# Token-major query features and a deferred layer-norm scale in a four-layer linear-attention and GLU kernel

## The chip, the cores and the metric

The kernel runs on one core of a Trainium2 chip. The metric is the device time in microseconds of that core; the median of several executions is quoted. The engines are called PE (TensorE matmul), PEld (its weight load), DVE (VectorE), ACT (ScalarE), POOL (GpSimd) and SP (SyncE, which here does nothing but issue DMAs). The granted clock is the share of PE's full clock that the profile shows as passed by the throttle. The record marks an execution as slow when it is over 1.5% above the fastest of the same kernel.

## The reference, cut to what matters

2048 tokens (16 tiles of 128), width 512, 32 heads of 16, GLU width 1376, bf16. Layers 1 and 3 are attention, 2 and 4 are GLUs; every layer reads a layer norm of x and adds to x.

```python
phi_q = concat([softmax(pq), softmax(-pq)], -1)     # pq = q @ w_phi per head, 16 -> 32 features
phi_k = concat([softmax(pk), softmax(-pk)], -1)
kv  = einsum("bhsf,bhsd->bhfd", phi_k, v);  z = einsum("bhsf->bhf", phi_k)
num = einsum("bhqf,bhfd->bhqd", phi_q, kv)
den = einsum("bhqf,bhf->bhq", phi_q, z)[..., None] + 1e-6
o   = (num / den) @ wo
...                                                  # GLU: (relu(x @ Wg) * (x @ Wu)) @ Wd
x = x + A(ln(x)); x = x + B(ln(x)); x = x + A(ln(x)); x = x + B(ln(x))
```

`kv` sums over all tokens. So each attention layer has a barrier: nothing of `num` can start before the last tile's k features have been accumulated. The stretch from that last accumulation to the first GLU matmul is called the boundary here; there are two, near 54 to 72 us and near 239 to 257 us.

## The kernel before

The program records every operation with its reads and writes in a list. A list scheduler then orders each engine's instructions by a model of their durations; a priority grows with the place in the emission, so what is emitted earlier tends to run earlier. Twenty stored steps of a random search improve that order. The program hands each engine, and the SP queue of DMA issues, its instructions in that order.

```python
# before: q is projected feature-major (features on partitions, tokens along the free dimension),
# so exp(q) can be the weights of num at once. A softmax sum over features is then a sum over
# partitions, which num computes itself: 144 columns = 128 of kv, 8 of den, 8 of the softmax sums.
op("pe", matmul(pb[bank][:, j*GW:(j+1)*GW], expq[:, st, c, s, tt*128:(tt+1)*128], kvbd[:, g0+j, :]))  # GW = 144
...                       # 3 evictions per tile, then zm, zd, zr, ab, tsc, o on POOL and DVE
self.dma_tr(dma_start_transpose(oT[:, ob, :, :], osb[:, b, :]), ...)    # o of one tile, on the SP queue
for c in range(NC):
    op("pe", matmul(pb[bank][:], oT[:, ob, c, :], wo_p[:, c, :]), ...)
op("dve", tensor_tensor(x_sb[:, t, :], x_sb[:, t, :], pb[bank][:], ALU.add), ...)
...
def ln(t): stats, aggregate, rstd = (var + eps)^-0.5, y = (x - mean) * rstd, then dma_tr(yT <- y)
...
# order of emission in each attention layer
N([0, 1, 2, 3])                                       # num .. wo and layer norm of tiles 0 to 3
for st in range(1, NSLAB):
    self.q_proj(st, qring, A, ...)                    # q projection and exp of tiles 4 to 15
mix(steps_B([0, 1], HA), steps_N([4, 5]))             # GLU of tiles 0, 1 between N of 4, 5
...
```

All transposes in DMA (`dma_tr`) go through the one SP queue: 60 of y (the normalised x), 32 of o and 11 others, besides most of the loads and stores.

The softmax here doesn't subtract the row's maximum and nothing guards it: scores larger than these inputs give would overflow.

## Time and profile before

| | before |
|---|---|
| time, median | 394.94 us (393.89 to 395.74) |
| span of the profiled execution | 391.6 us, granted clock 0.999 |
| PE, DVE, ACT, POOL busy | 94%, 68%, 51%, 43% |

The page of the profile: busy time by engine; then PE's busy tenths and the granted clock in 40 equal slices; then the DMA queue of SP; then the engines' shares of the chain that ended last.

```profile
PE 369.0 (94%) x2336; PEld 201.8 (52%) x2379; DVE 268.1 (68%) x551; ACT 201.5 (51%) x381; POOL 170.2 (43%) x287
...
PE   5898988999999999999999997979999999999996
...
PEclk9999999999999999999999999999999999999999
...
q1 hardware_dynamic: 65328, 23.07, 26.3%
...
PE 84%; DMA 5%; DVE 4%; ACT 3%; issue 2%; POOL 1%; SPq 0%; POOLq 0%; DVEq 0%
```

PE is the bound: it works 94% of the span at full clock and makes up 84% of the chain. The two groups of the page that the change touches most (busy us, mean ns of one; then the idle time before them and its releaser):

```profile
L774 PE MATMUL ps<-wo_p,oT 128*128 128x512 bf16 x117 | 35.3, 379 | 3.9 <-DMA oT<-osb 3.5
...
L743 PE MATMUL ps<-kvbd,expq 128*128 128x144 bf16 x256 | 33.6, 226 | 2.4 <-DVE kvbd L716 2.1
```

A matmul's 226 ns isn't the spacing, since the next one starts before it ends. The timeline shows three num matmuls in a row in 0.35 us, so the spacing is (0.35 - 0.226) / 2 = 62 ns.

The table of stretches (us from start to end; busy us of PE, PEld, DVE, ACT, POOL; granted clock; DMA share; GB/s) at the two boundaries:

```profile
60.00:70.00 10.00, 8.82 (x57) 4.40 (x56) 8.60 (x22) 8.64 (x13) 3.97 (x10) 1.00 0.20 42
70.00:80.00 10.00, 9.04 (x78) 6.41 (x78) 8.42 (x22) 7.67 (x16) 7.98 (x18) 1.00 0.36 70
80.00:90.00 10.00, 9.57 (x68) 6.48 (x69) 8.05 (x20) 3.38 (x10) 5.17 (x10) 1.00 0.34 69
...
250.00:260.00 10.00, 6.89 (x48) 3.78 (x47) 7.85 (x17) 7.87 (x12) 7.01 (x14) 1.00 0.32 57
260.00:270.00 10.00, 9.95 (x89) 7.83 (x90) 7.85 (x22) 5.94 (x17) 6.46 (x14) 1.00 0.29 59
```

PE loses at most about three microseconds in a stretch of ten, and the clock stays at 1.00.

### The profile page before, as it was taken

Reading aid. Unit: us, or ns where it says so; the run is one execution under the profiler, and the core shown is the slowest. Engines: PE = TensorE matmul, PEld = TensorE weight load, DVE = VectorE, ACT = ScalarE, POOL = GpSimd, SP = SyncE. Lnnn points to the kernel's source line nnn. Section 1 sums busy time; section 2 is a strip of 40 time slices with the busy share of each in tenths; the row PEclk is TensorE's granted clock in tenths of the full one; section 3 lists DMA queues with packets and bytes.
Section 4 is the critical chain, followed back from the end, with each engine's and each line's share of the span. In section 5 each row is a group of like instructions: output and inputs, shape, how many; then the busy total and the mean of one; then the engine's idle time right before and its main releaser. Section 6 shows DMA issues by size and latency. Waiting matters only on the chain.

```text
span 391.6 us, 6419 instructions
## 1 busy us (share of the span) xinstructions
PE 369.0 (94%) x2336; PEld 201.8 (52%) x2379; DVE 268.1 (68%) x551; ACT 201.5 (51%) x381; POOL 170.2 (43%) x287
## 2 busy tenths in 40 slices
PE   5898988999999999999999997979999999999996
PEld 4444444576744554454444464456774445454443
DVE  5989878887766889766675776978875676322222
ACT  5787869742643413534354475965652561443340
POOL 7597952771543383533433652466544252000000
PEclk9999999999999999999999999999999999999999
DMA  6752492332221225301110120233233123100001
GB/s 195 195 80 57 114 364 53 70 65 47 54 51 29 41 54 83 68 2 27 27 15 0 27 28 2 41 62 68 62 69 79 27 43 83 41 13 15 27 28 55
DMA packets 66080, 24.08 MB, mean 61 GB/s; under 512 B 57888, under 2 KB 65024, under 8 KB 66048
## 3 DMA queue, kind: packets, MB, share of 16 engines
q1 hardware_dynamic: 65328, 23.07, 26.3%
q10 hardware_dynamic: 720, 0.59, 0.5%
q8 instruction: 19, 0.31, 0.4%
q14 instruction: 13, 0.11, 0.1%
HBM read 7.91 MB, written 2.10 MB: 26 GB/s over the span
## 4 chain that ended last, share of the span: by engine, by line
PE 84%; DMA 5%; DVE 4%; ACT 3%; issue 2%; POOL 1%; SPq 0%; POOLq 0%; DVEq 0%
PE ps L795 34%; PE ps L844 19%; PE ps L654 9%; PE ps L774 6%; PE ps L727 5%; PE ps L685 3%; PE ps L743 3%; PE ps L821 2%; DMA oT<-osb 2%; PE ps L699 2%; DMA yT<-ytile 1%; ACT expq L730 1%; DMA x_sb<-in_A_x_dram 1%; DVE tsc L763 1%; ACT expk L688 0%
## 5 line engine op out<-in xcount | busy, mean ns | idle before, releaser
L795 PE MATMUL ps<-yT,Wgu 128*128 128x512 bf16 (+1 forms) x789 | 173.8, 336 | 0.5
L795 PEld LDWEIGHTS ps<-yT,Wgu 128*128 128x128 bf16 x800 | 75.7, 98 | 62.0 <-ACT expk L803 1.4
L844 PE MATMUL ps<-Wd,hT 128*128 128x512 bf16 (+2 forms) x356 | 103.5, 373 | 0.4
L797 ACT ACTIVATE gate_sb<-ps 128x512 bf16<-128x512 f32 (+1 forms) x100 | 50.4, 513 | 82.7 <-PE ps L795 71.8
L673 POOL TENSOR_TENSOR expk<-expk,rZk 128x1024 bf16<-128x1024 bf16 (+1 forms) x32 | 59.6, 1876 | 33.1 <-DVE rZk L668 27.6
L844 PEld LDWEIGHTS ps<-Wd,hT 128*128 128x128 bf16 (+1 forms) x363 | 35.2, 98 | 35.8
L805 DVE TENSOR_TENSOR hT<-gate_sb,expk 128x512 bf16<-128x512 bf16 (+1 forms) x65 | 26.8, 422 | 29.4 <-ACT expk L803 23.4
L588 DVE BATCH_NORM_STATS2 stats<-x_sb 128x6 f32<-128x512 bf16 x64 | 42.6, 680 | 4.8 <-DMA x_sb<-in_A_x_dram 4.2
L401 ACT ACTIVATE numbf<-ps 128x432 bf16<-128x432 f32 x64 | 33.0, 539 | 20.1 <-PE ps L743 19.5
L666 DVE TENSOR_REDUCE Zk<-expk 128x64 f32<-128x1024 bf16 x32 | 38.1, 1205 | 4.5 <-ACT expk L688 2.6
L846 DVE TENSOR_TENSOR x_sb<-x_sb,ps 128x512 bf16<-128x512 bf16 (+1 forms) x33 | 22.0, 670 | 26.8 <-PE ps L844 26.6
L768 POOL TENSOR_TENSOR osb<-tsc 128x512 bf16<-128x512 bf16 x28 | 32.3, 1155 | 17.6 <-DVE tsc L763 17.6
L774 PE MATMUL ps<-wo_p,oT 128*128 128x512 bf16 x117 | 35.3, 379 | 3.9 <-DMA oT<-osb 3.5
L727 PE MATMUL ps<-yT,Wqp 128*128 128x512 bf16 x123 | 34.6, 379 | 2.3 <-ACT expq L730 2.1
L730 ACT ACTIVATE expq<-ps 128x1024 bf16<-128x1024 f32 (+1 forms) x40 | 32.2, 861 | 7.2 <-PE ps L727 5.9
L743 PE MATMUL ps<-kvbd,expq 128*128 128x144 bf16 x256 | 33.6, 226 | 2.4 <-DVE kvbd L716 2.1
L595 POOL TENSOR_SCALAR rv<-mv 128x1 f32<-128x1 f32 (+1 forms) x53 | 12.6, 240 | 53.6 <-DVE mv L590 53.1
L803 ACT ACTIVATE expk<-ps 128x512 bf16<-128x512 f32 (+1 forms) x65 | 32.2, 501 | 6.3 <-PE ps L795 6.2
L596 POOL TENSOR_TENSOR rstd<-rv,mhalf 128x1 f32<-128x1 f32 (+1 forms) x53 | 31.5, 597 | 3.0
L631 DVE TENSOR_SCALAR ytile<-x_sb,mv,rstd 128x512 bf16<-128x512 bf16 x52 | 22.1, 426 | 12.4 <-POOL rstd L596 11.7
L754 POOL TENSOR_TENSOR zm<-numbf 128x64 f32<-128x64 bf16 x28 | 10.5, 375 | 45.8 <-DVE numbf L401 33.0
L657 ACT ACTIVATE expk<-ps 128x512 bf16<-128x512 f32 x44 | 23.7, 603 | 12.5 <-PE ps L654 12.0
(78 smaller groups left out, 428.9 us busy)
## 6 DMA issues: line engine op xcount, KB each, us to landing
out_dram<-x_sb SPq DMA_DIRECT2D x15, 128.0 KB, 1.7
x_sb<-in_A_x_dram SPq DMA_DIRECT2D x3, 512.0 KB, 6.4
Wgu<-in_B_W_gate_dram SPq DMA_DIRECT2D x4, 344.0 KB, 4.0
Wgu<-in_B_W_up_dram SPq DMA_DIRECT2D x4, 344.0 KB, 5.9
Wd<-in_B_W_down_dram SPq DMA_DIRECT2D x5, 256.0 KB, 7.7
yT<-ytile SPq DMA_TRANSPOSE x60, 2.5
hT<-in_A_wqkv_dram ACTq DMA_DIRECT2D x4, 128.0 KB, 3.0
x_sb<-in_A_x_dram SPq DMA_DIRECT2D x4, 128.0 KB, 3.5
```

Of the source, the lines that this page charges most:

```text
L401: return e.activation(out, in_, ACT.Copy) if hasattr(e, "activation") else e.tensor_copy(out, in_)
L588: op("dve", (lambda t: lambda e: e.bn_stats(k.stats6[:, t, :], k.x_sb[:, t, :]))(t), [r("x", t)], [r("st", t)], 685, f"{tag} stats {t}")
L654: op("pe", (lambda ic, bank, W: lambda e: e.matmul(k.pb[bank][:], k.yT[:, ic, t * 128:(t + 1) * 128], W[:, ic, :], start=(ic == 0), stop=( ...
L666: op("dve", lambda e: e.tensor_reduce(k.Zk[:, zb, :], k.expk[:, t, :, :, :].rearrange("p g s (h f) -> p (g s h) f", f=16), AX.X, ALU.add), ...
L673: op(eng, (lambda kv, u0, n: lambda e: e.tensor_tensor(kv, kv, k.rZk[:, rb, u0 * 32:u0 * 32 + n].unsqueeze(2).to_broadcast([P, n, 16]), AL ...
L727: op("pe", (lambda c, ic, bank: lambda e: e.matmul(k.pb[bank][:], k.Wqp[:, ic, c * 128:(c + 1) * 128], k.yT[:, ic, st * 512:(st + 1) * 512 ...
L730: op("act", (lambda c0, s, b0: lambda e: e.activation(k.expq[:, st, c0:c0 + w, s, :], k.ps[:, b0:b0 + w, :], ACT.Exp, scale=(1.0 - 2.0 * s ...
L743: op("pe", (lambda s, c, j, g0, bank: lambda e: e.matmul(k.pb[bank][:, j * GW:(j + 1) * GW], k.expq[:, st, c, s, tt * 128:(tt + 1) * 128], ...
L774: op("pe", (lambda c, bank: lambda e: e.matmul(k.pb[bank][:], k.oT[:, ob, c, :], k.wo_p[:, c, :], start=(c == 0), stop=(c == NC - 1)))(c, ...
L795: op("pe", (lambda bank, W, ic, fc, Mf: lambda e: e.matmul(k.pb[bank][0:Mf, 0:n], W[:, ic, fc * 128:fc * 128 + Mf], k.yT[:, ic, c0:c0 + n] ...
L797: op("act", (lambda Mf, gb, gs: lambda e: e.activation(k.gate_sb[0:Mf, gs, 0:n], k.pb[gb][0:Mf, 0:n], ACT.Relu))(Mf, gb, gs), [self.RP[gb] ...
L844: op("pe", (lambda fc, Kf, u, c0, bank, m0, m1: lambda e: e.matmul(k.pb[bank][:, m0:m1], k.hT[0:Kf, u, c0:c0 + 128], k.Wd[0:Kf, fc, m0:m1] ...
```

## The change

Two things are changed. First, q is projected token-major. The softmax sums are then ordinary sums along the free dimension, and num shrinks from 144 to 68 columns (4 heads of 16 and their den). But num contracts over features, so the features must be transposed back: two DMA transposes of 128x512 per tile and layer, 64 in all. Second, the layer norms before layers 2 to 4 are deferred: `512 x - sum(x)` is transposed at once, while the scale is computed beside it and enters later, at the exp, at the copy of v, or at the GLU's residual (relu(s g) * (s u) = s^2 relu(g) u). The stored search steps, which belonged to the old program, are gone. Smaller things come with it: the ring of oT has 3 buffers instead of 4, and num keeps one pair of PSUM banks for every tile.

```diff
-    STEPS = (540311766, 892937877, ... 18 more ...)
+    STEPS = ()
-GW = 144
+HW = 17
+GW = 4 * HW
...
-    def q_proj(self, st, ring, tag, after=(), w=1):      # out = Wqp^T @ yT : feature-major
+    def q_proj(self, ts, ring, tag, scaled=False):       # out = yT^T @ Wqp : token-major
...
+        for tt in ts:
+            self.qnorm(tt, tag)
+    def qnorm(self, t, tag):
+        op("dve", tensor_reduce(Zq[:, b, :], expq[:, t, ...], AX.X, ALU.add), ...)
+        op("dve", reciprocal(rZq, Zq of exp(q)), ...)
+        op("pool", tensor_tensor(rho, rZq, Zq of exp(-q), ALU.mult), ...)
+        for u in range(2):
+            op("pool", tensor_tensor(exp(q) half u, same, rho, ALU.mult), ...)
+            self.dma_tr(dma_start_transpose(qT[:, tb, u*4:u*4+4, :], expq[:, t, u*4:u*4+4, :, :]), ...)
...                                                        # num: 8 matmuls of 68 columns from qT
-        # three evictions, zm, zd, zr, ab, tsc, o
+        op("dve", reciprocal(rden, den in PSUM), ...)
+        op("dve", tensor_tensor(osb, num in PSUM, rden, ALU.mult), ...)
...
+    def center(self, t, tag, power):
+        op("dve", tensor_scalar(ytile, x, 512., sx, op0=ALU.mult, op1=ALU.subtract), ...)
+        self.dma_tr(dma_start_transpose(yT[...], ytile), ...)
+        op("act", activation(sq, x, ACT.Square, scale=-512., bias=sx, accum_out=vx), ...)
+        ...                                                # rx = (vx/512 + eps*512^2)^power on POOL
...
             N([0, 1, 2, 3])
-            for st in range(1, NSLAB):
-                self.q_proj(st, qring, A, ..., w=2)
+            for t in range(4, NT, 2):
+                self.q_proj([t, t + 1], qring, A, last)    # with qnorm and both transposes of t, t+1
             mix(steps_B([0, 1], HA), steps_N([4, 5]))
```

## The prediction

> **What bounds the kernel now.** TensorE. The page gives PE 369.0 us of a 391.6 us span (94%) at granted clock 0.999, and the chain that ended last is 84% PE. From 90 to 220 us and from 260 to 380 us the table of stretches shows PE busy 9.9 of every 10 us. PE idles at the start, at the first attention-to-GLU boundary (50-90 us: 4.2 us), at the second (220-260 us: 5.5 us) and in the tail. DVE, ACT and POOL have slack on average, but in 36-54 us POOL is busy 16.2 and DVE 15.4 of 18 us.
>
> **Removed from PE.** The 256 "num" matmuls shrink from 144 to 68 columns. In the timeline six in a row take 0.54 us, the first 0.226, so 63 ns apiece; 27 k-v accumulations of 65 columns with their own 128-column weights take 0.86 us, 32 ns apiece. So 256 x 31 ns = 8 us less. Given back: four eps matmuls (0.5 us), and 68 instead of 65 columns (0.3 us). Net about 7 us, nearly all on the chain.
>
> **Moved on the other engines (estimates from the group means).**
> - ACT loses 64 num evictions (33 us), gains 48 Square passes of about 0.9 us and slower one-tile exps with a per-row scale: +20 us, mostly where it has room.
> - DVE loses num casts 14, tsc 22, zr 11, and stats and aggregation for 48 tiles (41); gains Zq 39, rZq 11, rden 13, o from PSUM 22, row sums 4: about even.
> - POOL: slightly less.
> - SP gains 64 transposes at 1.19 us of issue each (+76 us on 121), 2.4 us to land.
>
> **The chains at the boundaries.** From the last k-v accumulation to the GLU: eight mask operations (2.4 us) become two, the seven steps from num to o become two (rden 0.42, o 0.7), and stats, aggregate, rv and rstd (1.7 us) leave: 3 to 5 us shorter per boundary. That isn't all gained, since q projections fill PE meanwhile.
>
> Second boundary: gain 2 to 3 us. First: about nothing, perhaps a loss, because the q normalisation of the first tiles (1.55 us DVE, 1.5 us POOL each) enters a stretch where both are full, and its transposes share the SP queue with 6 MB of late weights issued at 41-54 us (DMA share 0.98 in 50-60 us). The Trainium skill, "DMA: Bandwidth & Descriptors", section on queues, rings and completion order says descriptors on one engine's ring are consumed in order; a transpose behind the weights would land only at about 60 us.
>
> **Against it.** The twenty schedule-search steps, tuned for the old program, are gone: my guess is a loss of 1 to 4 us (no number in the trace sizes it).
>
> **Sum.** 395 - 7 (num) - 2.5 (second boundary) + 0.5 (first) + 2.5 (lost search) - 1.5 (shorter waits elsewhere) = about 387 us. 80% range 380.5 to 393.5. Chances: faster by over 2% 0.5, within 2% 0.46, slower by over 2% 0.04: the middle lies right on the border.
>
> **What would show it.** Num matmuls near 32 ns apiece; PE busy sum down by 7 to 15 us; PE still 9.9 of 10 in the GLU stretches; PE idle at the second boundary below 4 us; first num at 58-61 us instead of 56.8, waiting on a q transpose.
>
> **What would make it wrong.** A table load for each Square (1.28 us each); transposes queueing on SP so that num or wo waits for DMA in the GLU stretches; num's two banks, now held per tile until DVE has read them, stalling PE; a much worse order without the search; or, the other way, boundaries closing wholly (380 us).

## More of the kernel before

The SP queue at the first boundary, from the timeline (start us, time on the queue, line, what is issued, how many):

```profile
53.91 0.50 SPq L579 DMA_DIRECT2D Wd<-in_B_W_down_dram  x1
61.31 7.79 SPq L771 DMA_TRANSPOSE oT<-osb  x3
69.69 2.50 SPq L634 DMA_TRANSPOSE yT<-ytile  x2
72.58 4.36 SPq L771 DMA_TRANSPOSE oT<-osb  x2
```

Only seven transposes are issued from 54 to 76.9 us, and the queue rests in between.

## The result, and the profile after

The kernel after took 423.79 us (median of 4, 422.6 to 424.91) against 395.26 us for the kernel before in the same rounds. The ratio is 1.0727, 95% interval 1.0687 to 1.0768: slower. A ratio here is the mean time of one kernel's fast runs over that of the other's of the same rounds, so it is not quite the ratio of the medians quoted. The prediction of 387.0 us (380.5 to 393.5) was wrong in size and in direction.

The page after, the same lines:

```profile
PE 374.1 (89%) x2343; PEld 195.1 (46%) x2383; DVE 255.2 (60%) x507; ACT 215.0 (51%) x421; POOL 158.9 (38%) x288
...
PE   5898976399799999999999999739998999999996
...
PEclk9999999689899999999999999957999999999999
...
q1 hardware_dynamic: 100080, 31.47, 37.6%
...
PE 62%; DVE 15%; DMA 10%; SPq 5%; issue 3%; ACT 3%; POOL 2%; DVEq 0%; ACTq 0%
```

No engine is busier as a share of the span. What changed is that PE has two holes, in slices 7 and 8 and in slices 26 and 27, and that the granted clock falls with or just after them (slices 8 and 9, and 27 and 28; a third, smaller dip is in slice 11). SP's own queue, 0% of the chain before, is 5% of it, and DMA has doubled.

The groups: num costs 18.0 us of busy time instead of 33.6 (eight in a row take 0.41 us, so the spacing is (0.41 - 0.194) / 7 = 31 ns, as predicted). The new idle time stands before wo and before the GLU's first block, and both wait for a DMA transpose:

```profile
L804 PE MATMUL ps<-wo_p,oT 128*128 128x512 bf16 x125 | 39.5, 406 | 12.3 <-DMA oT<-osb 11.7
...
L850 PE MATMUL ps<-Wgu,yT 128*128 128x192 bf16 x128 | 17.4, 260 | 11.6 <-DMA yT<-ytile 11.6
```

PE's waits (what waited, for what: us in all, times, the longest) say how long each lasts:

```profile
PE ps L804 <- DMA oT<-osb: 11.7, 7, 5.3
PE ps L850 <- DMA yT<-ytile: 11.6, 6, 3.1
```

The stretches at the two boundaries:

```profile
60.00:70.00 10.00, 6.21 (x59) 3.20 (x60) 6.54 (x12) 4.57 (x5) 5.60 (x11) 1.00 1.00 207
70.00:80.00 10.00, 5.16 (x26) 1.62 (x24) 8.12 (x20) 5.01 (x9) 6.23 (x15) 0.88 0.47 93
80.00:90.00 10.00, 5.68 (x34) 3.95 (x35) 6.00 (x12) 2.30 (x7) 2.29 (x6) 0.61 0.65 105
...
270.00:280.00 10.00, 3.29 (x17) 1.08 (x16) 8.27 (x18) 4.43 (x10) 5.14 (x12) 0.78 0.50 95
280.00:290.00 10.00, 6.80 (x33) 4.53 (x35) 3.35 (x9) 2.88 (x9) 1.49 (x4) 0.54 0.60 91
```

And SP's queue at the first boundary:

```profile
66.80 1.27 SPq L801 DMA_TRANSPOSE oT<-osb  x1
68.17 2.51 SPq L783 DMA_TRANSPOSE qT<-expq  x2
70.74 1.26 SPq L801 DMA_TRANSPOSE oT<-osb  x1
72.17 2.50 SPq L783 DMA_TRANSPOSE qT<-expq  x2
74.72 1.27 SPq L801 DMA_TRANSPOSE oT<-osb  x1
76.09 2.52 SPq L783 DMA_TRANSPOSE qT<-expq  x2
78.66 1.26 SPq L668 DMA_TRANSPOSE yT<-ytile  x1
80.01 2.53 SPq L783 DMA_TRANSPOSE qT<-expq  x2
82.60 1.26 SPq L668 DMA_TRANSPOSE yT<-ytile  x1
```

Between two o transposes, and again between two y transposes, stand two q transposes for tiles that nobody needs yet, and the queue never rests: one start follows the other at 1.3 us. The o of a tile therefore comes every 3.9 us, and the GLU gets its first y at 81 us. The DMA engines themselves are half idle meanwhile (share 0.47 to 0.65). The queue that issues is full, and what lies behind it is not.

The holes then cost twice. The Trainium skill, "TensorE: Matmul & The Clock Gate", section "Part 1: The HAM clock gate", says that PE falls to half clock after an idle window of about 3.4 us and needs a busy one to come back. The trace agrees in kind, but not on the length. Stretches of one microsecond at the edges of the two large falls (the column before the last two is the clock):

```profile
77.00:78.00 1.00, 0.73 (x3) 0.36 (x4) 0.69 (x1) 0.42 (x2) 0.76 (x3) 0.81 0.63 130
78.00:79.00 1.00, 0.86 (x3) 0.00 (x0) 0.10 (x1) 0.00 (x0) 0.33 (x1) 0.50 0.40 81
...
87.00:88.00 1.00, 1.00 (x7) 0.56 (x5) 0.00 (x0) 0.50 (x2) 0.00 (x0) 0.57 0.30 62
...
275.00:276.00 1.00, 0.00 (x0) 0.00 (x0) 1.00 (x3) 0.00 (x0) 0.92 (x3) 0.80 0.31 61
...
289.00:290.00 1.00, 1.00 (x10) 0.84 (x9) 0.25 (x1) 1.00 (x4) 0.00 (x0) 0.88 0.67 130
```

At the first boundary the clock falls to 0.50 at 77.6 us, just after a wait of 2.5 us (it ended at 77.3), and is back at 87.9; the wait of 3.1 us, from 82.0 to 85.1, lies inside the fall and didn't start it. At the second it falls at 275.6 us, 3.7 us into the wait of 5.3 us, and is back at 289.2. A third fall, from 108.3 to 111.8 us, begins as a wait of 2.6 us ends. So waits shorter than the page's window were enough here. The slowest wo matmul takes 634 ns where the kernel before has at most 390. The half clock is most of why PE's busy time rose to 374.1 us although its work shrank: e18 below, with the same matmuls at full clock, has 366.4 us.

Where the span grew by 30.5 us, in milestones (start of each in the trace, us; the last two rows are explained below):

| | last k-v sum, layer 1 | first GLU matmul, layer 2 | last k-v sum, layer 3 | first GLU matmul, layer 4 | end |
|---|---|---|---|---|---|
| before | 54.1 | 72.2 | 238.8 | 256.6 | 391.6 |
| after | 62.8 | 81.2 | 260.8 | 281.2 | 422.1 |
| e7 | 59.3 | 76.5 | 242.3 | 254.8 | 386.9 |
| e18 | 59.5 | 74.0 | 243.6 | 256.6 | 388.8 |

From before to after: 8.7 us up to the first milestone, 0.3 to the second, 13.0 to the third, 2.5 to the fourth and 6.0 to the end. The loss isn't inside the boundary alone: while the backlog of q transposes lasts, the GLU that follows is starved too (PE busy 7.13 of 10 us at 100 to 110 us). A milestone isn't a fixed amount of PE's work, since the scheduler may move projections across it; the table says when, not why.

The 8.7 us before the first milestone are another loss than the queue at the boundary. From 33.5 to 54.4 us the chain of waits of the kernel after runs through DVE: the softmax sums of k, those of the first q tiles, and y. In the kernel before it is PE's own work for most of that time.

### The profile page after: what moved, and what is told of

It reads as the page before. It is cut to its first block, busy times and chain, and to the rows that moved or that the text cites. A ratio compares the mean times of both kernels' runs of the same rounds, so it can differ in the third digit from the quotient of the medians.

```text
span 422.1 us, 6512 instructions
## 1 busy us (share of the span) xinstructions
PE 374.1 (89%) x2343; PEld 195.1 (46%) x2383; DVE 255.2 (60%) x507; ACT 215.0 (51%) x421; POOL 158.9 (38%) x288
## 4 chain that ended last, share of the span: by engine, by line
PE 62%; DVE 15%; DMA 10%; SPq 5%; issue 3%; ACT 3%; POOL 2%; DVEq 0%; ACTq 0%
PE ps L824 27%; PE ps L873 16%; PE ps L804 6%; PE ps L683 6%; DVE Zq L772 4%; DMA yT<-ytile 4%; SPq L783 4%; DMA oT<-osb 4%; DVE Zk L696 2%; PE ps L850 2%; DVE stats L593 2%; PE ps L755 2%; PE ps L791 1%; PE ps L715 1%; POOL expk L703 1%
## 5 line engine op out<-in xcount | busy, mean ns | idle before, releaser
L826 ACT ACTIVATE gate_sb<-ps 128x512 bf16<-128x512 f32 (+1 forms) x100 | 50.4, 511 | 86.5 <-PE ps L824 78.7
L670 ACT ACTIVATE sq<-x_sb,sx 128x512 bf16<-128x512 bf16 x48 | 34.7, 724 | 47.1 <-DVE x_sb L657 42.6
L804 PE MATMUL ps<-wo_p,oT 128*128 128x512 bf16 x125 | 39.5, 406 | 12.3 <-DMA oT<-osb 11.7
L875 DVE SCALAR_TENSOR_TENSOR x_sb<-ps,rx,x_sb 128x512 bf16<-128x512 f32 (+1 forms) x33 | 24.1, 732 | 35.1 <-PE ps L873 30.5
L772 DVE TENSOR_REDUCE Zq<-expq 128x64 f32<-128x1024 bf16 x32 | 38.1, 1203 | 3.3 <-POOL rho L777 2.8
L780 POOL TENSOR_TENSOR expq<-expq,rho 128x256 bf16<-128x256 bf16 x64 | 39.1, 631 | 0.9
L657 DVE SCALAR_TENSOR_TENSOR x_sb<-ps,x_sb 128x512 bf16<-128x512 f32 x32 | 21.9, 685 | 23.1 <-PE ps L804 21.3
L755 PE MATMUL ps<-Wqp,yT 128*128 128x512 bf16 x123 | 33.1, 379 | 2.4 <-ACT expq L764 2.0
L683 PE MATMUL ps<-Wkp,yT 128*128 128x512 bf16 x85 | 28.4, 388 | 2.2 <-DMA yT<-ytile 1.2
L837 DVE TENSOR_TENSOR hT<-gate_sb,ps 128x512 bf16<-128x512 bf16 (+1 forms) x35 | 20.9, 603 | 13.5 <-PE ps L824 12.5
L683 PE MATMUL ps<-wv_p,yT 128*128 128x512 bf16 x85 | 28.1, 379 | 0.2
L850 PE MATMUL ps<-Wgu,yT 128*128 128x192 bf16 x128 | 17.4, 260 | 11.6 <-DMA yT<-ytile 11.6
```

What stands on the lines that cost most here:

```text
L670: op("act", lambda e: e.activation(k.sq[:], k.x_sb[:, t, :], ACT.Square, scale=-float(D), bias=k.sx[:, t, :], accum_out=k.vx[:, t, :]), [r ...
L683: op("pe", (lambda ic, bank, W: lambda e: e.matmul(k.pb[bank][:], k.yT[:, ic, t * 128:(t + 1) * 128], W[:, ic, :], start=(ic == 0), stop=( ...
L755: op("pe", (lambda ic, bank, tt: lambda e: e.matmul(k.pb[bank][:], k.yT[:, ic, tt * 128:(tt + 1) * 128], k.Wqp[:, ic, :], start=(ic == 0), ...
L772: op("dve", lambda e: e.tensor_reduce(k.Zq[:, b, :], k.expq[:, t, :, :, :].rearrange("p g s (h f) -> p (g s h) f", f=16), AX.X, ALU.add), ...
L780: op("pool", (lambda ev, u: lambda e: e.tensor_tensor(ev, ev, k.rho[:, b, u * 16:u * 16 + 16].rearrange("p (g h) -> p g h", h=4).unsqueeze ...
L804: op("pe", (lambda c, bank: lambda e: e.matmul(k.pb[bank][:], k.oT[:, ob, c, :], k.wo_p[:, c, :], start=(c == 0), stop=(c == NC - 1)))(c, ...
```

## The experiments

Theories. **T**: the 64 added transposes on the one in-order SP queue, emitted ahead of the first GLU's o and y, starve PE. Rivals: **R1**, the lost search made a bad order; **R2**, the deferred scale; **R3**, the q normalisation on DVE and POOL (1.5 us each per tile), not its transposes. Ratios are to the kernel before in the same rounds. Savings between two runs are differences of their medians; taken from the ratios they differ by up to 1.5 us, because not all runs were in the same rounds. All kernels passed the comparison with the reference, those that are wrong too: its tolerance doesn't notice wrong attention features, so "correct" says little about them.

### e1: the kernel before without its search

```diff
-    STEPS = (540311766, 892937877, ...)
+    STEPS = ()
```

> The old kernel with its twenty search steps taken out, nothing else. Theory 'lost search' (my recorded guess: 1 to 4 us, perhaps more): if the search were what the new kernel misses, this one must lose most of 28 us, so over 410 us. Theory 'order of the q normalisation' and theory 'extra work' expect no such thing: 395 to 400 us.

Measured: 395.15 us, ratio 1.0031 (0.999 to 1.0072). R1 falls for the old program: the stored search was worth about 1 us, perhaps nothing. Whether a search of its own would have helped the kernel after as it stands wasn't tried.

### e2: the deferred scale alone, before the GLUs

The kernel before with `center` in place of `ln` ahead of layers 2 and 4; q stays feature-major, no search. To fit in memory the ring of oT has 3 buffers instead of 4, and the Square's unused output is 8-bit.

> The old kernel without search, with the deferred scale in front of the two GLUs alone (centre, Square on ScalarE, scale at the residual); query features stay feature-major, layer norm before the second attention stays as it was. Theory 'deferred scale costs' (Square passes on ACT, sums on DVE): slower than e1, over 405 us. The theories that blame the token-major queries expect e1 or a little better, 390 to 398 us, because the chain at each boundary is 1.7 us shorter.

Measured: 396.84 us (median of all four), ratio 0.9995 (0.9914 to 1.0075). Two of the four executions were slow and are left out of the ratio; the two fast ones, 391.77 and 395.93 us, lie 4 us apart. R2 falls as a cause of a loss of 28 us. On its own the deferral moves nothing that can be seen within that interval.

### e3: token-major q alone

```diff
-                    self.center(t, L1, -1)
+                    self.ln(t, L1)
...                                # likewise for layer 3, the residual and the scales at exp and v
```

> The new kernel with the layer norms undone (statistics and scale applied before the transpose, as in the old kernel); token-major queries stay. Theories 'order of the q normalisation' and 'extra work of the q path' expect it as slow as the new kernel or slower, 422 to 435 us, since statistics add DVE time to the crowded stretches. Theory 'deferred scale costs' expects it near 395 us.

Measured: 431.46 us, ratio 1.0947 (1.0909 to 1.0985). The whole loss comes with token-major q. The deferral gives back 431.46 - 423.79 = 7.7 us of it. A likely reading, not tested by itself: where the chain to the GLU is exposed, a shorter chain pays; where it is hidden (e2), it doesn't.

### e4: the same instructions, q normalisation and its transposes emitted later

```diff
             def N(ts, norm=True):
                 for t in ts:
+                    if norm and t + 2 < NT:
+                        self.qnorm(t + 2, A)      # two tiles ahead of its num
                     self.num(t, (6, 7), wring, A)
...
             for t in range(4, NT, 2):
-                self.q_proj([t, t + 1], qring, A, last)
+                self.q_proj([t, t + 1], qring, A, last, norm=False)
+            for t in range(4, 6):
+                self.qnorm(t, A)
```

> The new kernel with the same instructions, but the normalisation and transposes of query tiles 4 to 15 handed to the scheduler two tiles ahead of the tile's num, instead of all before the GLU; projections and exps stay where they were. Theory 'order': DVE, POOL and the SP queue are free for the first tiles at both boundaries, PE idle at each falls below 6 us, granted clock above 0.99 in all slices, 388 to 402 us. Theory 'extra work': the work only moves, 415 us or more. Theory 'lost search': 415 us or more, since no search is added.

Measured: 407.35 us, ratio 1.0332 (1.0289 to 1.0375). Not one instruction is taken away, and 16.4 us are gone. The time lies between the two outcomes stated (388 to 402 us, or 415 and more): place is much of the loss, but not all. The second boundary, 20.4 us long after, is 14.0 us long, and the GLU's waits for y fall from 11.6 to 0.8 us. But the waits for o did not vanish. They have become shorter and more, and moved into the GLU stretches:

```profile
PE ps L804 <- DMA oT<-osb: 16.0, 12, 2.9
```

### e5 and e6: the kernel after in its exact order, with one part left out

Both leave operations out after the scheduling, so that every remaining instruction keeps its place. e5 leaves out the 48 q transposes of tiles 4 to 15 (wrong: num reads the first tiles' features). e6 leaves out all of q's normalisation on DVE and POOL and keeps all 64 transposes (wrong: features not normalised).

```diff
+        gone = {o.idx for o in ops if self.left_out(o.name.split())}
+        order = [o for o in order if o.idx not in gone]
...                                # left_out: e5 "qtr" of tiles 4 to 15; e6 "Zq", "rZq", "rho", "phiq"
```

> Wrong result on purpose. The new kernel in exactly its own order, with the 48 query transposes of tiles 4 to 15 left out at emission (the first four tiles keep theirs); normalisation stays. If the SP queue of transposes is what delays the first tiles' o and y transposes, the PE waits on transposes (23 us in the new kernel) mostly vanish and the time falls to 395 to 405 us. If DVE and POOL time of the normalisation is the cause, it stays above 412 us.

> Wrong result on purpose. The new kernel in exactly its own order, all 64 query transposes kept, but the query normalisation of all 32 tiles (sum, reciprocal, ratio, two products: about 49 us of DVE and 48 of POOL) left out. If DVE and POOL time is the cause: last k-v accumulation of the first attention back from 62.8 to about 55 us, total 395 to 405 us. If the SP queue is: the transposes still stand in the same order, each 1.27 us, total above 410 us.

Measured: e5 406.8 us, ratio 1.0313 (1.0271 to 1.0355); e6 422.0 us, 1.0696 (1.0651 to 1.0741). Taking away the transposes saves 17.0 us (1.8 us above the range stated for T, 5 us under the one for R3); taking away all the arithmetic that feeds them saves 1.8 us. In e6 the waits for o and y are as long as after (10.3 and 12.6 us). T stands, and R3 falls as the first bound. It isn't nothing, though: in e5, 12 us are still missing, and the stretch from 70 to 80 us there has DVE busy 9.75 of 10 us and PE 6.05. The sums of q for tiles 4 to 15 are emitted just as early as their transposes, and with the queue free, DVE is the next thing that they clog (e7 tests this). Nor does e6 move the first milestone, which is at 63.1 us: with the q sums gone from DVE, PE waits there for a y transpose that took 4.9 us to land, among the weight loads.

### e7: e4 and e5 together

> Wrong result on purpose. The late-normalisation kernel e4 (407 us) in its own order, without the 48 query transposes of tiles 4 to 15. If what remains in e4 after the ordering is repaired is the SP queue (PE waits 16 us in total for o transposes, spread over the GLU stretches), it falls to 388 to 396 us. If it is the added DVE, ACT and POOL work or the first k-v stretch, it stays above 400 us.

Measured: 389.18 us, ratio 0.9865 (0.9825 to 0.9906). The normalisation is all there, at a later place; 48 transposes are missing. Against e4 that is 18.2 us for 48 transposes. Against e5, which lacks the same transposes, it is 17.6 us for the place of the normalisation alone: early normalisation is a second bound of the same size, hidden as long as the queue is full (e6). 389.2 us lies within the predicted range, but in part by luck, since the terms don't match one by one: the row of e7 in the table above shows the first GLU matmul 4.3 us later than before (predicted 0.5) and the second boundary at 12.5 us instead of 17.9 (predicted 2 to 3 us gained). PE is full from 80 us on except at the second boundary (9.63 and 8.21 of 10 us at 240 to 260); what is left is at the first boundary (PE 7.59 and 6.49 of 10 us at 50 to 70).

### e8: e4, with the attention steps spread evenly over the GLU blocks

```diff
-                mix(steps_B([2, 3], HA), steps_N([6, 7, 8]))
-                mix(steps_B(tiles(1), HA), steps_N([9, 10, 11, 12, 13]))
+                mix(steps_B([2, 3], HA), steps_N([6, 7]))
+                mix(steps_B(tiles(1), HA), steps_N([8, 9, 10, 11]))
...
```

> Correct result. e4 with the attention steps of tiles 4 to 15 spread evenly over the GLU blocks of each layer (two tiles beside each of the first two blocks, four beside the third, four beside the fourth) instead of nearly all in the first half, so that about four transposes of 1.27 us fall on every 7 us of GLU time. If the SP queue is only crowded locally: 390 to 400 us. If the scheduler pulls the steps forward anyway or the cost is elsewhere: 405 to 410 us as e4.

Measured: 403.93 us, ratio 1.0248 (1.0192 to 1.0303), 3.4 us below e4 and between the two outcomes stated; the waits for o fall from 16.0 to 11.0 us. A lower density of transposes helps some.

### e9 and e11: one q transpose of 128x1024 per tile instead of two of 128x512

```diff
-            self.dma_tr(dma_start_transpose(qT[:, tb, u*4:u*4+4, :], expq[:, t, u*4:u*4+4, :, :]), ...)   # u = 0, 1
+        self.dma_tr(dma_start_transpose(qT[:, tb, :, :], expq[:, t, :, :, :]), ...)
```

e9 does this in e4, e11 in the kernel after with its emission otherwise untouched.

> Correct result. e4 with one query transpose of 128x1024 per tile in place of two of 128x512: the same bytes, half as many DMA instructions on SP. If a transpose holds the SP queue for a fixed time per instruction (the 128x256 one of the GLU tail holds it 1.25 us, as long as a 128x512 one), it holds it about 1.3 us, 40 us of SP time go, and the time falls to 392 to 399 us. If the time goes with the bytes, it holds it about 2.5 us and nothing or little is gained: 403 to 410 us.

> Correct result. The new kernel, order of emission untouched, with one query transpose of 128x1024 per tile in place of two of 128x512. If the number of transposes on the SP queue is the root of the loss, halving the 64 added ones takes back a good part of the 17 us that leaving 48 of them out took back: 408 to 416 us. If only their place in the order matters, it stays at 418 to 425 us.

Measured: e9 398.88 us, 1.0088 (1.0043 to 1.0133); e11 410.88 us, 1.0439 (1.04 to 1.0479). The same bytes in half the instructions save 8.5 us and 12.9 us. So it is the number of transposes, not their bytes, that fills the queue. SP's time per transpose, from the instructions on the tile qT (shortest, median and longest in ns), of e4:

```profile
L783 SPq DMA_TRANSPOSE qT<-expq x64: 1188/1267/2413, 51.0 to 319.0; - x64
```

and of e9, with twice the bytes in each:

```profile
L783 SPq DMA_TRANSPOSE qT<-expq x32: 1231/1310/2146, 53.7 to 304.7; - x32
```

Twice the bytes cost 43 ns more on the queue. Landing grows from 2.5 to 3.3 us. So the number of the transposes is shown by itself, by e5, e9 and e11. Their place is shown by e4 and e6 together: e4 moves the normalisation along with its transposes, but while the transposes stay early, even leaving the normalisation out (e6) gains only 1.8 us.

### e10: e4, with the weights for layer 2 behind the last transposes of layer 1

The loads of wo, Wg and Wu wait for the last y transposes of layer 1's norm, those of Wd for the q transpose of tile 3.

> Correct result. e4 with the late weights moved in the SP queue: wo, Wg, Wu wait for the layer-norm transposes of tiles 14 and 15 both, Wd waits for the query transpose of tile 3. If the weights ahead of the query transposes cost the first boundary (in e4 a query transpose took 5.7 us at 63 us, first GLU matmul at 78.7 us against 72.2 in the old kernel), the first GLU matmul comes at 72 to 76 us and the total falls by 3 to 6 us to 401 to 405. If the weights don't matter there, it stays at 406 to 409.

Measured: 404.61 us, ratio 1.0268 (1.0217 to 1.0319). The first GLU matmul comes 5 us earlier (73.7 instead of 78.7 us), but only 2.7 us reach the end. Presumably a shift of the first boundary is partly lost again while the queue limits the GLU stretches.

### e12 to e16: the repaired kernel, and why it isn't faster still

e12 combines e9, e8 and e10, makes q's features one tile ahead of num instead of two, gives the scheduler the measured queue times (1.27 and 1.31 us), and has a search of its own. (The expectation says 31 search steps; the kernel had 17.)

> Correct result, meant to beat both kernels: query normalisation one tile ahead of its num, one transpose per tile, Wd behind the query transpose of tile 3, attention steps spread over the GLU blocks, the transpose times in the scheduler's table set to those measured (1.27 and 1.31 us), 31 search steps. If the SP queue was the whole of the loss, what the change saves on TensorE (7 us) shows at last: 384 to 391 us against 395. If something else in the new query path costs, it ends at 393 or more.

Measured: 395.59 us (6 runs), ratio 1.0055 (1.0012 to 1.0098). It only equals the kernel before, outside the 384 to 391 us stated for the case that SP's queue was the whole of the loss. The second boundary is now better than the old one (PE 8.07 of 10 us in its worst stretch, where the kernel before has 6.89); at the first, SP's queue had put wo, Wg and Wu right ahead of the first q transpose:

```profile
53.88 0.60 SPq L585 DMA_DIRECT2D Wgu<-in_B_W_up_dram  x1
54.52 9.26 SPq L786 DMA_TRANSPOSE qT<-expq  x4
67.55 1.19 SPq L805 DMA_TRANSPOSE oT<-osb  x1
```

The first of the four took 8.3 us to land, and PE waited 5.5 us for it. So the obvious suspect was the weights. e13 is e12 without the search; e14 is e13 with Wg and Wu held back until the q transpose of tile 1 has landed; e15 is e14 with a search; e16 is e15 with the features two tiles ahead again and its own search.

```diff
-        for piece in pieces[:12]:                # wo, Wg, Wu
+        for piece in pieces[:4]:                 # wo
             piece(self.r("yT", 14))
...
         self.q_proj([0, 1], qr0, "A0")
+        for piece in pieces[4:12]:               # Wg, Wu
+            piece(self.r("qT", 1, 1))
```

> The program of e12_repaired with the order of the list scheduler, without the 17 search steps. If the search's choice made the first boundary bad (it put the weights ahead of the first q transpose), this is at or below 1.0055; if the search helped as it did in the old kernel, it is about 1.01 (398 to 400 us).

> e13 with one change: the eight loads of Wg and Wu may start only after the q transpose of tile 1. Theory (the weights ahead of the first q transposes hold them up by 5 us or more): the first q transposes land in under 4 us each, the first num comes before 63 us, and the time is 4 to 9 us below e13 (about 389 to 393 us). Rival (VectorE, full from 40 to 60 us with the normalisation of the first tiles, is what the first boundary waits for): within 2 us of e13.

> e14 with 15 steps of order search. The search gave 0.3 % in the old kernel (e1). If that holds, 1 to 2 us below e14, so about 388 to 391 us, a ratio of 0.982 to 0.992.

> e15 with the q features of a tile made two tiles ahead of its num instead of one, and its own 13 search steps. If one tile ahead is too late for the transpose (3.3 us to land), this is 1 to 3 us faster than e15; if more transposes ahead of the first o transposes cost again, it is 2 to 5 us slower.

Measured:

| | median us | ratio, 95% interval |
|---|---|---|
| e13 | 392.38 | 0.995 (0.9909 to 0.9991) |
| e14 | 392.47 | 0.9959 (0.9917 to 1.0002) |
| e15 | 394.01 | 0.9992 (0.9946 to 1.0038) |
| e16 | 398.31 | 1.0106 (1.005 to 1.0162) |

Two more expectations failed. The search didn't help: e12 is 3.2 us slower than e13, and e15 1.5 us slower than e14 (these two intervals overlap). A likely reason, not tested by itself: the model that it optimises gives a transpose one landing time, so its choice at the first boundary (weights ahead of the transposes) costs nothing in the model. And holding back the weights didn't help either: the suspect of e12 was real in e12, but in e14 the time is that of e13, which by the expectation speaks for the rival named there, DVE (e17 tests it). e14's chain of waits shows why not all was gained: the weights were no longer behind the y transpose of tile 14, so this one was issued at 48.8 us behind three weight loads and took 4.6 us to land. One waiter had been exchanged for another. Two tiles ahead (e16) is 4.3 us slower than one (e15), but each had its own search, so not all of this need be the lookahead.

### e17 and e18: the last two suspects at the first boundary

e17 is e15 in its exact order without the normalisation of q tiles 0 to 3 in layer 1 (wrong). e18 is e14 with wo, Wg and Wu behind the y transpose of tile 14 again.

```diff
-    ... [rd, r("yT", 15)], [r(nm, c)] ...
+    ... [rd, r("yT", 14), r("yT", 15)], [r(nm, c)] ...
```

> e15 in its exact order, with the normalisation (sum, reciprocal, ratio, product: VectorE and GpSimd) of q tiles 0 to 3 of the first layer left out at emission; their q transposes stay. Wrong on purpose. If the full VectorE and GpSimd bound the first boundary, 3 to 6 us below e15 (388 to 391 us); if not, within 1.5 us of it.

> e14 with the loads of wo, Wg and Wu also behind the transpose of tile 14, which they overtook in e14. If that 4.6 us wait held the first boundary, the transpose lands in 2.5 us and the time is 2 to 4 us below e14 (388.5 to 390.5 us); if another chain ends just behind it, within 1 us of e14.

Measured: e17 392.72 us, ratio 0.9958 (0.9921 to 0.9994), 1.3 us below e15, so by its own criterion the normalisation isn't what holds this boundary. It isn't a clean test: its queue times shifted, and three q transposes took 9.65 us on the queue behind the weights. e18: 390.97 us (6 runs, 390.32 to 391.61), ratio 0.9924 (0.9901 to 0.9947); 1.5 us below e14, between the two stated outcomes; the intervals of the two ratios overlap.

e18 is 0.8% under the kernel before, by an interval that excludes 1, and about 7.5% under the kernel after. The first is under the 2% that a verdict of faster needs, so against the kernel before the verdict is "same"; e18 is also the best of a dozen variants. Its page:

```profile
PE 366.4 (94%) x2383; PEld 193.0 (50%) x2383; DVE 253.5 (65%) x507; ACT 215.5 (55%) x421; POOL 158.9 (41%) x288
...
PEclk9999999999999999999999999999999999999999
```

The clock is full everywhere again, and PE's share is back at 94%. Against the kernel before, by the milestones: 5.4 us later at the first, then 3.6 gained, 3.1 lost, 5.0 gained at the second boundary and 2.7 gained to the end. What makes the first attention stage 5.4 us longer is open; in e18 too the chain from 40 to 54 us runs through DVE's softmax sums of k and q. The place of the weights and the normalisation of its first tiles were each tried; each moved the end by 1.5 us at most, and another wait took its place. A version without the q transposes of these tiles was not run.

## Why the prediction was wrong, point by point

**The step that failed** is the line "SP gains 64 transposes at 1.19 us of issue each (+76 us on 121), 2.4 us to land". The count and the time of one were right (1.22 us at the median after, 1.27 in e4). But the sum was entered as a load of an engine with room, 197 of 400 us, and no term of "395 - 7 - 2.5 + 0.5 + 2.5 - 1.5" holds it. It would have been clear: per layer, 24 q transposes of tiles 4 to 15 are emitted ahead of the first GLU step, 24 x 1.19 = 28.6 us on an in-order queue, at a boundary that lasts 18 us in the trace before and on whose chain two more kinds of transpose, o and y, use the same queue. The trace after shows just that: PE waited 11.7 us for o and 11.6 us for y, where the kernel before waited 3.5 us for o. e5, e7, e9 and e11, and e4 with e6, show it by experiment. "Transposes queueing on SP so that num or wo waits for DMA in the GLU stretches" was listed among the things that could make it wrong, and "slower by over 2%" was given 0.04. A risk that a product of two read numbers can size belongs in the sum.

**A second thing overlooked** is what a hole in PE's work costs: the half clock after it. The kernel before shows none in its working stretches (a clock of 1.00 in all), so nothing in its profile pointed there; the Trainium skill, "TensorE: Matmul & The Clock Gate", section "Part 1: The HAM clock gate", did.

**Num from 63 to 32 ns apiece**: right (62 and 31 ns measured), and so is 8 us for 256 of them.

**ACT, DVE, POOL**: ACT rose 13.5 us (predicted 20), DVE fell 12.9 (predicted about even), POOL fell 11.3 ("slightly less"). The Square cost 0.72 us and 0.19 us for reading its accumulator, as predicted (0.9). None of these mattered.

**Boundary chains 3 to 5 us shorter, second boundary 2 to 3 us gained**: right as a mechanism, hidden in the kernel after. With the queue freed, the second boundary shrinks from 17.9 to 12.9 us (e18) and 12.5 us (e7). That is 5.0 and 5.4 us gained, more than the 2 to 3 predicted.

**First boundary +0.5 us, with transposes behind the weights that land at about 60 us**: this term was mis-sized too. The first GLU matmul came 9.0 us later (81.2 instead of 72.2), 8.7 us of it before the last k-v sum, where DVE was full (19.75 of 20 us at 40 to 60), as the prediction had warned. The first num came at 61.8 us, a little after the 58 to 61 stated, and waited for DVE (`kvbd`), not for a q transpose. The prediction drew the landing time from the Trainium skill, "DMA: Bandwidth & Descriptors", section "Queues, rings and completion order". e12 shows it in the open: issued at 54.5 us behind the weights, landed at 62.8. But it isn't the main thing that made the kernel after slow: holding the weights back gained 2.7 us in e10 and nothing from e13 to e14. (The late weights are 4640 KB by the page's table of issues, not 6 MB.)

**Lost search 1 to 4 us, 2.5 in the sum**: too high in the sum; e1 gives 1.2 us or nothing, and the new searches gained nothing.

**What would show it**: "PE still 9.9 of 10 in the GLU stretches" failed (7.13 at 100 to 110 us), "PE idle at the second boundary below 4 us" failed (from 270 to 290 us alone PE is idle for 9.9 us), and "PE busy sum down by 7 to 15 us" failed (up 5.1, with the half clock). In e18 it is down 2.6 us; the trace before lacks 43 matmul records (2336 matmuls against 2379 weight loads), so this difference is a lower bound rather than a measure.

## What to carry to other kernels

Treat a DMA queue as an engine: here it issued one thing after another, and each transpose of 128x256 to 128x1024 occupied it for 1.2 to 1.3 us (longer among weight loads: three took 9.65 us in e17), so count the instructions that a change puts on it between the first producer and the last consumer of each stage, and compare with the length of that stage, not with the whole span. If work for later tiles must share a queue with the chain of the first ones, emit it just ahead of its use, and join small transposes into large ones. When a bound is taken away, expect the next (here DVE behind the queue, then waits at the first boundary of which the last was not found), and judge a gain that was promised by one part of a change in a version in which that part isn't hidden.

## What the Trainium skill lacked or had wrong

- "DMA: Bandwidth & Descriptors", section "DMA Transpose (X-bar)": no word on what an issued transpose costs its queue, and no section gives it for transposes of these shapes on this chip. Here a 128x512 transpose holds SP's queue for 1.19 us at least and 1.27 us at the median in a full queue (e4), a 128x1024 one for 1.23 and 1.31 us (e9): nearly constant, so the rate is set by the number of instructions. It lands 2.5 and 3.3 us after issue.
- "Advanced Engine Details and Errata", section "X-Bar Transpose (TRN2)", says that transpose DMAs are as fast as regular ones, with 350 to 400 GB/s expected. No stretch here comes near it: with the queue full of 128x512 transposes it moved 91 to 105 GB/s at a DMA share of 0.47 to 0.65 (the kernel after, 70 to 90 and 270 to 290 us), which is 150 to 200 GB/s at full share by our estimate. In e11, with transposes of 128x1024, it moved 209 GB/s with the engines full (a share of 1.11, 258 to 259 us), while the plain weight loads of the kernel before moved 343 GB/s at a share of 0.98 (50 to 60 us).
- "TensorE: Matmul & The Clock Gate", section "Back-to-back issue gap", gives 131 ns per matmul of 512 columns and 81 ns for 128 in a stream with weight loads, and calls the formula N / 2.4 + 2.5 an isolated gap. Here the formula holds in the stream, with new weights for each: 31 ns at 68 columns, 62 ns at 144, 215 ns at 512 (three in 0.81 us, one in 0.38). Other sections of the page have the formula for back-to-back matmuls, and these agree with the numbers here.
- The same page's "Part 1: The HAM clock gate" was missed by the prediction and is right about the half clock (0.50 in three falls of the kernel after). Its idle window of about 3.4 us isn't the least wait that suffices: two of the falls came at the end of waits of 2.5 and 2.6 us.
